# Top-k attention with a SMeLU MLP: the scores of two steps in one visit, with the values of two steps between them

## The chip, the cores and the metric

One core of one Trainium2 chip runs the whole program. The metric is the device time of one execution in microseconds (us). The kernel before has a median of 1504.06 us over three runs (1502.19 to 1506.8).

The engines named below each run their own queue of instructions in order: TensorE (PE for matmuls, PEld for weight loads), VectorE (DVE), ScalarE (ACT), GpSimd (POOL) and SyncE (SP), which here issues all the DMAs.

## The reference

```python
B, H, S, D = 8, 8, 576, 64                      # q, k, v: float32, (B, H, S, D)
scores = (1 / sqrt(D)) * q @ k.T                # per batch and head, (S, S)
kth    = np.partition(scores, -32)[..., -32]    # the 32nd largest of each row
scores = np.where(scores >= kth, scores, -1e9)
attn   = exp(scores - rowmax);  attn /= attn.sum(-1) + 1e-9
x      = (attn @ v).transpose(0, 2, 1, 3).reshape(4608, 512)
h      = x @ w_in                               # (512, 2048)
g      = h if h >= 1, 0 if h <= -1, else (h + 1)**2 / 4
out    = g @ w_out                              # (2048, 512)
```

## The kernel before

**Steps and rounds.** The unit of attention work is a *step*: a tile of queries and two heads, so two blocks of 128 rows of 576 scores. A query tile (a *round*) has four steps, one for each pair of heads. A batch has four tiles of 128 queries and a tail of 64; the tails of two batches are handled in rounds of two steps, each with four heads. Eight batches make 144 steps. Four steps fill one `xT` tile of 128 tokens by 512 features (a *chunk*), 36 in all, on which the MLP runs.

**One step.** TensorE multiplies queries by keys into two PSUM buffers (`scores`, L354), ScalarE evicts each half into `s` in SBUF with the scale (L355). VectorE finds the 32nd largest of each row: it folds each row into the larger and the smaller of two halves (`more`, `less`, L368), takes eight maxima at a time (L388, L416, L424, L435, L442) and strikes them out (L375). ScalarE makes the negative row maximum (`nmax`, L389) and the exponentials (L391) of the next step while VectorE works on this one. VectorE multiplies the exponentials by the mask and sums them (L454). GpSimd divides by the sum (L407). The weights then have to be turned for the second matmul: in the first eight steps and the last two TensorE does that (`transpose_w`, with `diag`, L404 and L469), in all others DMAs do (`move_w`): ScalarE splits the words into `halves` (L484), one DMA stores them as `rows` (L486), a transposing DMA brings them back as `wT` (L488). `values` multiplies `wT` by the values (L502, L510) and ScalarE copies the result into `xT` (L515, L517).

**The MLP.** `hidden` makes two blocks of 128 hidden units (eight matmuls, L535); ScalarE and GpSimd apply the activation (L539, L546, L551 to L553); `final` accumulates into `py` (L558). These pieces wait in the list `pending` and are put between the attention's instructions by `advance`.

**Early and late.** During the first eight steps (`early`) the weights are still converted to their form in SBUF, in slots of the same loop. The switch to the late order is at step 8.

**What sets the order.** The order on TensorE, VectorE, ScalarE and GpSimd is that in which the program calls the functions; only the queue of SP is ordered by the framework. The loop `for m in range(n + 2)` (L737) has seven slots for each step m. In slot 2 of an even late step the pending `hidden` pieces are drained, the values of steps m - 4 and m - 3 are made (`values_until`), and then the scores of step m + 2 (`begin_at`, L792). An odd late step makes only the scores of step m + 2. So TensorE leaves the MLP for attention twice in two steps. In slot 3 the weights of step m - 1 are moved. `advance` takes MLP pieces by a planned time for TensorE and VectorE.

**Queries and keys.** `queries(m + 3)` (L795) prepares a round's queries: for batches 0 and 1 TensorE transposes them, later `turn` (L275) does it as for the weights: ScalarE splits `q_in` into `parts`, a DMA stores `lines`, a transposing DMA fills `qT`. Then the load of the round after the next is issued into the buffer just read (two buffers `q_in`). The keys of the next batch come in the same way, one block every second step (`turned_keys_of`, `load_block`), each load issued ahead of the turn of the block before it (two buffers `k_in`); the keys of batches 0 and 1 are transposed by TensorE (`keys_of`, `load_keys`). Values come in by twelve loads for each batch (`load_values`, L194, L197, L202).

**Buffers that matter here.** `scores_of` and `weights_of` have three tiles each, taken by m modulo 3. PSUM tag `a` (scores, transposes) has two buffers, tag `ph` (hidden units, values) three, `py` one. `halves` has one buffer, `wT` four.

Of the kernel before, what the change touches and what calls it, by code (L numbers as in the profile page):

```python
# [11 lines left out]
F32 = mybir.dt.float32  # L12
# [10 lines left out]
LARGEST = 3.4028234e38  # L23
# [3 lines left out]
def kernel(  # L27
# [10 lines left out]
    nc = tc.nc  # L38
    B, H, S, D = q.shape
# [46 lines left out]
            nc.gpsimd.memset(x, 0.0)  # L86


    scores_of, weights_of = [[const.tile([P, 2, S + 8], F32, name=f"{x}{i}") for i in range(3)] for x in ("s", "e")]
    for i in range(3):  # L90
        nc.gpsimd.memset(scores_of[i][:, :, S:S + 1], LARGEST)
        nc.gpsimd.memset(weights_of[i][:, :, S:S + 1], 1e-9)

# [80 lines left out]
    def run(ctx, paired):  # L176
# [29 lines left out]

        def load_queries(b, t):
            if t < NT:
                q_in = stage.tile([P, H, D], F32, name="q_in", bufs=2)
                nc.sync.dma_start(out=q_in, in_=whole(q, b)[:, :, t, :])  # L210
            else:
                q_in = stage.tile([TL, H, D], F32, name="q_tl", tag="q_in", bufs=2)
                nc.sync.dma_start(out=q_in, in_=q[b, :, SM:S, :].rearrange("h p d -> p h d"))
            return q_in

# [18 lines left out]
        def keys_of(b):  # L234

            kT = stage.tile([P, NHP, S], F32, name="kT")
            k_tl = stage.tile([TL, H, D], F32, name="k_tl", bufs=1)
            got = dict(kT=kT)

            def load_keys(hp):  # L240
                k_in = stage.tile([P, NT, 2, D], F32, name="k_in")
                for j in range(2):
                    nc.sync.dma_start(out=k_in[:, :, j, :], in_=whole(k, b)[:, 2 * hp + j])
                return k_in

            k_in = load_keys(0)
            nc.sync.dma_start(out=k_tl, in_=k[b, :, SM:S, :].rearrange("h p d -> p h d"))
            yield got
            for hp in range(NHP):
                k_next = load_keys(hp + 1) if hp + 1 < NHP else None  # L250
                pt = ps.tile([P, NT, P], F32, name="pk", tag="a", bufs=2)
                for c in range(NT):
                    nc.tensor.transpose(pt[:, c, :], k_in[:, c].rearrange("p j d -> p (j d)"), ident)
                for j in range(2):
                    d = slice(j * D, (j + 1) * D)
                    copy = nc.vector.tensor_copy if b == 0 and hp < 2 and j else nc.scalar.copy
                    copy(kT[d, hp, main(j)], pt[d].rearrange("p c n -> p (c n)"))  # L257
                if hp == 0:
                    pt = ps.tile([P, NHP, TL], F32, name="pkt", tag="a", bufs=2)
                    for h2 in range(NHP):  # L260
                        nc.tensor.transpose(pt[:, h2, :], k_tl[:, 2 * h2:2 * h2 + 2].rearrange("p j d -> p (j d)"),
                                            ident[0:TL, 0:TL])
                    for j in range(2):
                        d = slice(j * D, (j + 1) * D)
                        copy = nc.vector.tensor_copy if b == 0 and j else nc.scalar.copy
                        copy(kT[d, :, tail(j)], pt[d])
                k_in = k_next
                if hp == NHP - 2:
                    loads = load_values(b)
                    got["v"], got["v_tl"] = next(loads)  # L270
                    for _ in loads:
                        pass
                yield got
# [16 lines left out]
        def turned_keys_of(b):  # L290

            kT = stage.tile([P, NHP, S], F32, name="kT")
            got = dict(kT=kT)

            def load_block(c):
                x = stage.tile([P, H, D], F32, name="k_block", tag="k_in")
                ends = k[b, :, SM:S, :].rearrange("h p d -> p h d")
                if c < NT:
                    nc.sync.dma_start(out=x[:, 0::2, :], in_=whole(k, b)[:, 0::2, c, :])
                    nc.sync.dma_start(out=x[TL:P, 1::2, :], in_=whole(k, b)[0:P - TL, 1::2, c, :])  # L300
                else:
                    nc.sync.dma_start(out=x[0:TL, 0::2, :], in_=ends[:, 0::2, :])
                nc.sync.dma_start(out=x[0:TL, 1::2, :], in_=whole(k, b)[P - TL:P, 1::2, c - 1, :] if c else ends[:, 1::2, :])
                return x

            blocks = {0: load_block(0)}
            got["loads"] = load_values(b)
            got["v"], got["v_tl"] = next(got["loads"])
            yield got
            for c in range(NT + 1):  # L310
                if c < NT:
                    blocks[c + 1] = load_block(c + 1)
                n = P if c < NT else TL
                turn(blocks.pop(c)[0:n], kT[:, :, c * P:c * P + n])
                yield got

        def turned_queries_of(q_in, t):
# [17 lines left out]

        def scores(st):
            t, hp, kT, qT = st["t"], st["hp"], st["keys"]["kT"], st["qT"]
            st["all"] = (scores_of[st["m"] % 3][:, :, 0:S + 1], weights_of[st["m"] % 3][:, :, 0:S + 1])
            st["s"], st["e"] = s, _ = [x[:, :, 0:S] for x in st["all"]]
            for hf in range(2):  # L340
                sp = ps.tile([P, 2, BANK], F32, name="sp", tag="a", bufs=2)
                c0, c1 = hf * SH, (hf + 1) * SH
                products = []
                for i in range(2):
                    for j in ([i] if t < NT else [0, 1]):
                        d = slice(j * D, (j + 1) * D)
                        g = hp if t < NT else hp + i
                        o = sp[:, i] if t < NT else sp[part(i, j), i]
                        products.append([(o[:, a0 - c0:a1 - c0], qT[d, g, :], kT[d, g, k0:k0 + a1 - a0])
                                         for a0, a1, k0 in pieces(i, j, c0, c1)])  # L350
                for some in zip_longest(*products):
                    for x in some:
                        if x is not None:
                            nc.tensor.matmul(*x, start=True, stop=True)  # L354
                nc.scalar.activation(s[:, :, c0:c1], sp[:, :, 0:SH], AF.Copy, scale=SCALE)  # L355
# [324 lines left out]
        def queries(m):  # L680
            nonlocal pe_time
            if m < n and steps[m][0:2] not in qTs:
                r = steps[m][0:2]
                if r[0] > 1:
                    qTs[r] = turned_queries_of(q_ins[r], r[1])
                else:
                    qTs[r] = queries_of(q_ins[r], r[1], nc.vector.tensor_copy if m == 0 else nc.scalar.copy)
                    pe_time += 0.5
                fetch(rounds.index(r) + 2)

        def begin(m):
            b, t, hp, ch, col = steps[m]
# [5 lines left out]
        def begin_at(m):  # L698
            nonlocal pe_time
            if m < n:  # L700
# [2 lines left out]
                pe_time += 1.15  # L703
                scored[m] = pe_time + 2.0

        for i in range(2):
            load(words, i)
        next(first)
        for i in range(2, len(room) or 2):
            load(words, i)  # L710
        fetch(1)
        queries(0)
        convert(12.0)
        begin_at(0)
# [22 lines left out]
        for m in range(n + 2):  # L737
# [22 lines left out]
            for slot in range(SLOTS):  # L760
# [26 lines left out]
                if slot == 2 and not early:  # L787
                    if m % 2 == 0:
                        while pending and taken is not None and taken.__name__ == "hidden" and take():
                            pass  # L790
                    values_until((m - 2) // 2 * 2)
                if slot == (4 if early else 2):  # L792
                    begin_at(m + 2)
                if slot == (6 if early else 1):
                    queries(m + 3)  # L795
                    if (m < n and prep is None and next_keys < B and steps[m][0] == next_keys - 1 and steps[m][1] >= 1
                            and (next_keys > 1 or converted == n_pieces)):
                        prep = (turned_keys_of if next_keys > 1 else keys_of)(next_keys)
                    if prep is not None and (m % 2 == 0 or next_keys == 1):
                        got = next(prep, None)  # L800
                        pe_time += 0.5 if next_keys < 2 else 0.0
                        if got is None:
                            prep, next_keys = None, next_keys + 1
                        else:
                            keys[next_keys] = got
                            value_loads = got.get("loads", value_loads)
                    elif value_loads is not None:
                        next(value_loads, None)
# [57 lines left out]
```

## Time and profile before

| what | value |
|---|---|
| median of three runs | 1504.06 us |
| profiled execution, its own time | 1504.76 us |
| its span, first to last instruction | 1503.0 us |
| mean granted clock of TensorE | 0.989 |
| PE busy | 1451.9 us, 97% |
| VectorE busy | 1413.6 us, 94% |
| ScalarE busy | 1159.2 us, 77% |
| GpSimd busy | 905.5 us, 60% |
| chain that ended last, by engine | PE 85%, DVE 6%, ACT 4% |

A busy share is an average over the span. Matmuls overlap, and their ends in the profile are modelled, so a full PE is not by itself a PE at its peak. A row of a timeline gives start, duration, engine, line of the kernel, operation, what is written from what is read with its shape, the number of instructions merged, and in brackets the idle time of the engine just before, with what ended it. A row of the waits gives who waited, for whom, the total in us, the number of times, and the longest.

### The profile page before, as it was taken

The page shows a single profiled execution, that of the slowest core. Times are in us where ns is not written, and L with a number is a line of the kernel's source. Part 1 is how long each engine was busy: PE and PEld are TensorE (multiplying, and loading weights), DVE is VectorE, ACT ScalarE, POOL GpSimd, SP SyncE. Part 2 cuts the span into 40 slices and gives each one's busy share as a digit, 9 for nine tenths or more (in the row PEclk, how much of TensorE's full clock was granted, in tenths as well). Part 3 has the DMA queues.
Part 4 walks back from the last instruction along what each step waited for, and adds up shares of the span by engine and source line. Part 5 has one row for each costly group of instructions (what it writes and reads, how often), then busy time and mean ns, then how long its engine had stood idle before and what let it go on. Part 6 is the DMA issues. An engine that isn't in the chain of part 4 may idle for free.

```text
span 1503.0 us, 32202 instructions
## 1 busy us (share of the span) xinstructions
PE 1451.9 (97%) x10755; PEld 1043.6 (69%) x10755; DVE 1413.6 (94%) x4392; ACT 1159.2 (77%) x2221; POOL 905.5 (60%) x1309
## 2 busy tenths in 40 slices
PE   6998899999999999999999999899999999999998
PEld 5665577677777777677777777667777777777675
DVE  6999999999999999999999999999999999999912
ACT  7986877777888887787778888678778888787632
POOL 3473466666666666566666666566666666666630
PEclk8999999999999999999999999999999999999999
DMA  8633667775677776776677887886667777655610
GB/s 253 203 116 106 166 162 197 193 185 165 169 197 186 200 196 189 211 191 177 161 195 197 194 201 172 198 223 184 164 188 186 201 186 180 169 159 140 144 24 17
DMA packets 510319, 260.94 MB, mean 174 GB/s; under 512 B 460992, under 2 KB 469184, under 8 KB 510144
## 3 DMA queue, kind: packets, MB, share of 16 engines
q1 hardware_dynamic: 510144, 258.80, 66.3%
q8 instruction: 87, 1.43, 0.4%
q14 instruction: 88, 0.72, 0.1%
HBM read 62.91 MB, written 102.63 MB: 110 GB/s over the span
## 4 chain that ended last, share of the span: by engine, by line
PE 85%; DVE 6%; ACT 4%; DMA 2%; issue 2%; POOL 0%; SPq 0%; ACTq 0%; POOLq 0%
PE ph L535 31%; PE py L558 31%; PE sp L354 10%; PE po L502 9%; DVE more L375 1%; PE po L510 1%; DMA rows<-halves 1%; PE pw L469 1%; DVE e L454 1%; DMA wT<-rows 1%; DVE more L368 1%; ACT halves L484 1%; ACT e L391 1%; ACT units L146 1%; DVE tops L416 0%
## 5 line engine op out<-in xcount | busy, mean ns | idle before, releaser
L535 PEld LDWEIGHTS ph<-xT,w_in 128*128 128x128 f32 x4608 | 547.4, 192 | 100.5 <-issue 78.0
L535 PE MATMUL ph<-xT,w_in 128*128 128x128 f32 x4608 | 556.8, 276 | 1.7 <-ACT xT L515 1.0
L558 PE MATMUL py<-w_out,g 128*128 128x512 f32 x1152 | 555.6, 602 | 1.0 <-ACT y L561 0.9
L551 POOL TENSOR_SCALAR r<-r 128x256 f32<-128x256 f32 x276 | 142.9, 518 | 453.9 <-ACT r L539 453.8
L375 DVE MATCH_REPLACE8 more<-tops,more 128x288 f32<-128x288 f32 x864 | 375.0, 437 | 0.0
L558 PEld LDWEIGHTS py<-w_out,g 128*128 128x128 f32 x1152 | 194.9, 190 | 166.4 <-issue 159.1
L484 ACT COPY halves<-e 128x1152 uint16<-128x1152 uint16 x268 | 293.6, 1143 | 15.6 <-DMA rows<-halves 15.6
L454 DVE SCALAR_TENSOR_TENSOR e<-s,kth,e 128x577 f32<-128x577 f32 x288 | 260.4, 939 | 2.6 <-ACT e L391 2.5
L553 POOL TENSOR_TENSOR g<-r,g 128x256 f32<-128x256 f32 x280 | 239.5, 855 | 22.0
L407 POOL TENSOR_SCALAR e<-e,rz 128x576 f32<-128x576 f32 x268 | 222.8, 841 | 13.4 <-DVE rz L400 13.4
L391 ACT ACTIVATE e<-s,nmax 128x576 f32<-128x576 f32 x288 | 222.6, 773 | 4.7
L539 ACT ACTIVATE r<-ph,half 128x256 f32<-128x256 f32 (+1 forms) x296 | 135.9, 459 | 116.0 <-PE ph L535 91.9
L355 ACT ACTIVATE s<-sp 128x576 f32<-128x576 f32 x288 | 171.9, 648 | 58.5 <-PE sp L354 57.1
L552 POOL TENSOR_TENSOR r<-r 128x256 f32<-128x256 f32 x276 | 191.0, 692 | 23.0
L354 PE MATMUL sp<-kT,qT 64*128 64x288 f32 x1024 | 163.1, 435 | 10.7 <-ACT kT L257 8.5
L502 PEld LDWEIGHTS po<-wT,v_in 128*64 128x64 f32 x2048 | 116.2, 139 | 61.1 <-ACT g L546 49.5
L502 PE MATMUL po<-wT,v_in 128*64 128x128 f32 x2048 | 141.3, 280 | 12.0 <-ACT g L546 8.6
L354 PEld LDWEIGHTS sp<-kT,qT 64*128 64x128 f32 x1024 | 89.5, 188 | 71.9 <-ACT r L539 29.6
L546 ACT ACTIVATE g<-ph,minus 128x256 f32<-128x256 f32 x280 | 130.0, 464 | 0.0
L416 DVE MAX8 tops<-more 128x8 f32<-128x288 f32 x288 | 125.4, 442 | 0.0
L368 DVE TENSOR_TENSOR more<-s 128x576 f32<-128x576 f32 x144 | 112.4, 781 | 12.3 <-ACT s L355 12.3
L368 DVE TENSOR_TENSOR less<-s 128x576 f32<-128x576 f32 x144 | 121.6, 845 | 0.0
(90 smaller groups left out, 1379.8 us busy)
## 6 DMA issues: line engine op xcount, KB each, us to landing
rows<-halves SPq DMA_DIRECT2D x134, 576.0 KB, 3.1
lines<-parts SPq DMA_DIRECT2D x48, 256.0 KB, 2.6
q_in<-in_q_dram SPq DMA_DIRECT2D x32, 256.0 KB, 3.9
v_in<-in_v_dram SPq DMA_DIRECT2D x32, 256.0 KB, 4.2
out_dram<-y SPq DMA_DIRECT2D x32, 256.0 KB, 2.9
raw<-in_moe_w_in_dram SPq DMA_DIRECT2D x32, 256.0 KB, 3.2
raw<-in_moe_w_out_dram SPq DMA_DIRECT2D x32, 256.0 KB, 3.3
kT<-in_moe_w_in_dram SPq DMA_DIRECT2D x8, 512.0 KB, 5.3
```

Of the source, the lines that this page charges most:

```text
L354: nc.tensor.matmul(*x, start=True, stop=True)
L368: nc.vector.tensor_tensor(out=x, in0=s[:, :, 0:SH], in1=s[:, :, SH:S], op=op)
L375: nc.vector.match_replace(out=st["rest"][:, i, :], in_to_replace=eight(st["tops"], i, r - 8), in_values=src[:, i, :], imm_value=LOWEST)
L391: nc.scalar.activation(e[:, i, :], s[:, i, :], AF.Exp, bias=nmax[:, i:i + 1])
L407: nc.gpsimd.tensor_scalar(st["e"][:, i, :], st["e"][:, i, :], rz[:, i:i + 1], 1.0, ALU.mult, ALU.mult)
L454: nc.vector.scalar_tensor_tensor(out=st["all"][1][:, i, :], in0=st["all"][0][:, i, :], scalar=last[i], in1=st["all"][1][:, i, :], op0=ALU. ...
L484: nc.scalar.copy(halves[:, :, i * S:(i + 1) * S], st["e"][:, i, :].bitcast(U16).rearrange("p (k t) -> p t k", t=2))
L502: nc.tensor.matmul(po[j * D:(j + 1) * D], v_in[:, h, c, :] if c < NT else v_tl[0][:, h, :], wT[:, block(j, c)], start=(c == 0), stop=(c == ...
L535: nc.tensor.matmul(ph[:, i], w_in[:, kk, f * P:(f + 1) * P], xT[:, kk], start=(kk == 0), stop=(kk == NK - 1))
L552: nc.gpsimd.tensor_tensor(out=r, in0=r, in1=r, op=ALU.mult)
L553: nc.gpsimd.tensor_tensor(out=g, in0=r, in1=g, op=ALU.add)
L558: nc.tensor.matmul(py[0], gs[f // group][:, f % group], w_out[:, f, :], start=(f == 0), stop=(f == NF - 1))
```

## The change

In a late step of even number the scores of step m + 2 are made first, then the values of two steps, then the scores of step m + 3; a late step of odd number makes none. A step's scores can then be written while those of three others are in use, so `scores_of` gets a fourth tile; `weights_of` keeps three. To find the room, `q_in` and `k_in` get one buffer each in place of two: a round's queries are turned two steps earlier (`queries(m + 5)`), the load issued after a turn is that of the next round and not of the one after it, and a key block is loaded after the turn of the block before it. For batch 0 the blocks of keys are loaded into `xT` tiles, which are not yet in use.

```diff
-    scores_of, weights_of = [[const.tile([P, 2, S + 8], F32, name=f"{x}{i}") for i in range(3)] for x in ("s", "e")]
+    scores_of, weights_of = [[const.tile([P, 2, S + 8], F32, name=f"{x}{i}") for i in range(bufs)]
+                             for x, bufs in (("s", 4), ("e", 3))]
...
-                q_in = stage.tile([P, H, D], F32, name="q_in", bufs=2)
+                q_in = stage.tile([P, H, D], F32, name="q_in", bufs=1)
...
             def load_keys(hp):
-                k_in = stage.tile([P, NT, 2, D], F32, name="k_in")
+                if b == 0:
+                    k_in = xtp.tile([P, NK, P], F32, name="xT").rearrange("p c (j d) -> p c j d", j=2)
+                else:
+                    k_in = stage.tile([P, NT, 2, D], F32, name="k_in", bufs=1)
...
-                k_next = load_keys(hp + 1) if hp + 1 < NHP else None
+                k_next = load_keys(hp + 1) if hp + 1 < NHP and b == 0 else None
...
-                k_in = k_next
+                k_in = load_keys(hp + 1) if hp + 1 < NHP and b else k_next
...
-                x = stage.tile([P, H, D], F32, name="k_block", tag="k_in")
+                x = stage.tile([P, H, D], F32, name="k_block", tag="k_in", bufs=1)
...
+                n = P if c < NT else TL
+                turn(blocks.pop(c)[0:n], kT[:, :, c * P:c * P + n])
                 if c < NT:
                     blocks[c + 1] = load_block(c + 1)
-                n = P if c < NT else TL
-                turn(blocks.pop(c)[0:n], kT[:, :, c * P:c * P + n])
...
-            st["all"] = (scores_of[st["m"] % 3][:, :, 0:S + 1], weights_of[st["m"] % 3][:, :, 0:S + 1])
+            st["all"] = (scores_of[st["m"] % 4][:, :, 0:S + 1], weights_of[st["m"] % 3][:, :, 0:S + 1])
...
-                fetch(rounds.index(r) + 2)
+                fetch(rounds.index(r) + 1)
...
+        def begin_until(m):
+            for x in range(len(state), m + 1):
+                begin_at(x)
...
-        fetch(1)
         queries(0)
...
+                    begin_until(min(m + 2, len(state)))
                     values_until((m - 2) // 2 * 2)
-                if slot == (4 if early else 2):
+                    begin_until(m + 3 - m % 2)
+                if slot == 4 and early:
                     begin_at(m + 2)
                 if slot == (6 if early else 1):
-                    queries(m + 3)
+                    queries(m + (3 if early else 5))
```

More of the change, by code (lines that the diff above doesn't have):

```diff
@@ L86 @@
             nc.gpsimd.memset(x, 0.0)
-    scores_of, weights_of = [[const.tile([P, 2, S + 8], F32, name=f"{x}{i}") for i in range(3)] for x in ("s", "e")]
-    for i in range(3):
-        nc.gpsimd.memset(scores_of[i][:, :, S:S + 1], LARGEST)
-        nc.gpsimd.memset(weights_of[i][:, :, S:S + 1], 1e-9)
+    scores_of, weights_of = [[const.tile([P, 2, S + 8], F32, name=f"{x}{i}") for i in range(bufs)]
+                             for x, bufs in (("s", 4), ("e", 3))]
+    for tiles, behind in ((scores_of, LARGEST), (weights_of, 1e-9)):
+        for x in tiles:
+            nc.gpsimd.memset(x[:, :, S:S + 1], behind)
     SPLIT = TOP_K // 2
@@ L208, in load_queries @@
             if t < NT:
-                q_in = stage.tile([P, H, D], F32, name="q_in", bufs=2)
+                q_in = stage.tile([P, H, D], F32, name="q_in", bufs=1)
                 nc.sync.dma_start(out=q_in, in_=whole(q, b)[:, :, t, :])
             else:
-                q_in = stage.tile([TL, H, D], F32, name="q_tl", tag="q_in", bufs=2)
+                q_in = stage.tile([TL, H, D], F32, name="q_tl", tag="q_in", bufs=1)
                 nc.sync.dma_start(out=q_in, in_=q[b, :, SM:S, :].rearrange("h p d -> p h d"))
```

## The prediction

> **What bounds the kernel now.** I read the engine totals first, then the same totals cut into stretches, then the list of waits, then the timelines of the engines over one pair of steps, last the stalls and the tail. The profiled execution took 1504.76 us (span 1503.0 and 1.8 around it); the median of the runs is 1504.06, so what I subtract from one holds for the other.
>
> Totals and two stretches (columns: window, its length, busy us of PE, PEld, DVE, ACT, POOL, granted clock, DMA share, GB/s):
>
> ```profile
> PE 1451.9 (97%) x10755; PEld 1043.6 (69%) x10755; DVE 1413.6 (94%) x4392; ACT 1159.2 (77%) x2221; POOL 905.5 (60%) x1309
> ...
> 400.00:600.00 200.00, 199.89 (x1498) 143.66 (x1497) 200.00 (x627) 164.59 (x313) 132.72 (x190) 1.00 0.76 195
> 800.00:1000.00 200.00, 194.46 (x1504) 140.06 (x1502) 195.29 (x608) 158.78 (x299) 125.28 (x182) 0.98 0.80 196
> ```
>
> Two engines are full at once in the steady state, TensorE and VectorE. Neither waits for the other. So I ask which one could go faster alone. VectorE's period is read from the starts of its first operation on a step's scores (`more<-s`): step 31 starts at 332.67 and step 59 at 600.66, 9.57 us a step; steps 100 to 140 give 9.57 too. The shortest steps, which repeat in every round of four, take 9.14. TensorE's period, from scores block to scores block four steps on, is 38.27 us = 4 x 9.57. Here is one pair's visit on TensorE, the odd step's scores after it, and VectorE and POOL at one spot:
>
> ```profile
> 703.55 1.02 PE L558 MATMUL py<-w_out,g 128*128 128x512 f32 x2
> 704.62 1.09 PE L502 MATMUL po<-wT,v_in 128*64 128x128 f32 x16
> 706.63 0.39 PE L502 MATMUL po<-wT,v_tail 128*64 128x128 f32 x4
> 706.95 1.24 PE L354 MATMUL sp<-kT,qT 64*128 64x288 f32 x8
> 708.12 1.12 PE L558 MATMUL py<-w_out,g 128*128 128x512 f32 x2
> 709.08 1.95 PE L535 MATMUL ph<-xT,w_in 128*128 128x128 f32 x16
> 714.46 1.24 PE L354 MATMUL sp<-kT,qT 64*128 64x288 f32 x8
> ```
> ```profile
> 697.00 1.27 DVE L454 SCALAR_TENSOR_TENSOR e<-s,kth,e 128x577 f32<-128x577 f32 x1
> 715.70 0.81 DVE L454 SCALAR_TENSOR_TENSOR e<-s,kth,e 128x577 f32<-128x577 f32 x1
> ```
> ```profile
> 696.53 1.12 POOL L553 TENSOR_TENSOR g<-r,g 128x256 f32<-128x256 f32 x1
> 705.46 0.73 POOL L553 TENSOR_TENSOR g<-r,g 128x256 f32<-128x256 f32 x1
> ```
>
> TensorE has no hole to speak of: its own work fills 38.27. VectorE's masked multiply takes 0.81 alone and 1.27 where POOL's add (0.73 alone, 1.12 here) lies over it. That stretch, 0.4 to 0.5 us an overlap, is all that separates 9.14 from 9.57. While TensorE was ahead, from step 13 (160.67) to step 24 (265.34), VectorE made 9.52 a step. So I take TensorE as the pace and VectorE as a follower that would take only 0.05 us less if it were let.
>
> The waits that VectorE does have, and one of their causes:
>
> ```profile
> DVE more L368 <- ACT s L355: 12.3, 7, 2.8
> PEld po L502 <- ACT g L546: 49.5, 51, 6.2
> ```
> ```profile
> 615.55 4.02 SPq L202 DMA_DIRECT2D v_tail<-in_v_dram  x6
> ```
> ```profile
> 622.75 2.21 ACT L484 COPY halves<-e 128x1152 uint16<-128x1152 uint16 x2 [2.66 <-DMA rows<-halves]
> ```
> ```profile
> 626.41 1.80 PE L502 MATMUL po<-wT,v_in 128*64 128x128 f32 x16 [2.81 <-ACT g L546]
> ```
> ```profile
> 632.44 0.98 DVE L368 TENSOR_TENSOR more<-s 128x576 f32<-128x576 f32 x1 [2.73 <-ACT s L355]
> ```
>
> Read down: six issues for value tails hold SP's queue 4 us, the store of `rows` goes out late, ScalarE waits to refill its one `halves` buffer, the hidden units' evictions queue behind that, the values find no PSUM buffer, and the scores that stand behind the values reach VectorE late. It happens once more at 978 (TensorE 5.41, VectorE 2.81).
>
> The tail decides who is paid:
>
> ```profile
> 1428.43 0.69 ACT L404 ACTIVATE diag<-ident,rz 128x128 f32<-128x128 f32 x2 [1.51 <-DVE seconds L442]
> ```
>
> TensorE waits 2.13 us for this `diag`, which waits for VectorE's last step; the 74 us from there to the end are the same instructions in both kernels. So only time that VectorE gains moves the end.
>
> **What the Trainium skill says.** *TensorEngine Tiling (Array Packing)*, Key Properties: changing the tiling mode, not just the tile, drains TensorE. The trace agrees: scores (64-row tiles), values (64-column tiles) and MLP (whole array) follow each other with holes of 0.10 us and more, worked out below. *GPSIMD Engine Reference*, Key points: POOL shares its SBUF interfaces with VectorE and contends with VectorE instructions that have two SBUF inputs. The trace agrees (1.27 against 0.81). *Perfetto Trace Analysis*, Optimization Strategy: repeated bubbles can mean too few buffers; here the one 1 us hole before `po` (51 times) is a PSUM buffer awaited.
>
> **The change, part by part.**
>
> *Order on TensorE.* In the instruction order of the two programs a pair was: values, values, scores, MLP, scores, MLP; it becomes scores, values, values, scores, MLP. The MLP matmuls between visits are the same in number (80 and 14, then 48 and 18, hidden and output). One second-layer matmul recurs every 0.43 us, so the two of 703.55 would be over at 704.41: MLP to values costs 0.21 here (0.10 at 683.54 to 684.50). Values to scores: four tails take 0.22, over at 706.85, scores at 706.95: 0.10. Scores to MLP: 708.12 to 709.08 is 0.96 for 0.86 of work: 0.10. MLP to scores the same 0.10. Before: 0.10 to 0.21 + 0.10 + 0.10 + 0.10 + 0.10 = 0.50 to 0.61. After: three of 0.10 and one scores-to-values, which no trace shows; between 0 and 0.20 (a drain with the next weights exposed), I take 0.10 as for its neighbours. Saved 0.10 to 0.21, with the unknown 0 to 0.31; I take 0.15 x 66 pairs = 10 us of TensorE, 0.08 a step. That allows 9.49; VectorE's free rate, 9.52, is met first. Over the 128 steps from 13 to 141: 0.05 x 128 = **-6.4 us**, 0 if it stays at 9.57, -10 if all passes.
>
> *Scores ahead of the values.* At both stalls the even step's scores no longer stand behind the late values; the odd step's come some 8 us earlier than now. Scores are ready 1.9 us before use at the tightest (708.93 for 710.82); that becomes 4.2 by the values' 2.33 us. The stall itself stays, I assume: the value-tail loads still come four in a row. Removed: 2.73 + 2.81 = **-5.5**; the two steps after each stall are long by 3.7 in all (10.97, 9.79, 10.98, 10.25 against 9.57), half of which I credit: **-1.9**. TensorE's lost time is covered by its new lead; without that cover the 8 us come back.
>
> *Evictions.* The second scores need both PSUM buffers of tag `a` free: first eviction 0.8 after its matmuls' start, both done by 2.0 (706.95, 708.94); the second scores start 1.17 + 2.33 = 3.5 later. Hidden, unless ScalarE is over 1.5 us behind. ScalarE's row maximum and exponentials of the next step now stand behind two more evictions at even steps: the second exponential, done at 712.61, comes near 714.2 and is wanted at 716.43 (the first 715.70). Hidden with 1.5 to 2 us to spare. Odd steps lose two evictions and gain the same. The fourth scores buffer lets this be written while VectorE still reads three; the memset of its guard column is 0.1 us in the lead-in.
>
> *Queries.* The turn (ScalarE copy 1.04, store, load of the next tile, DMA transpose of 1.25 on SP) moves two steps earlier at the same slot, once in four steps; SP issues the same number. With one `q_in` the next load waits for that copy, which the old load of the same buffer did too. It has four steps (two at the tails) for 3.9 us: nothing.
>
> *Key blocks.* Three issues (1.6 to 2.5 us of SP) move from ahead of the turn to behind its copy. SP would hold the `rows` store and `wT` behind them if the copy were late; the store of `lines` waits for that same copy already, so nothing. Landing 4 us, need 19 us later.
>
> *Start.* Batch 0 keys go to `xT` tiles, so all four blocks load at once, and a query load leaves the queue: no wait of VectorE shown there is on them; 0, between -2 and +2. At the switch (step 8) one query transpose and its copy (0.66 and 0.56) come ahead of the scores for which VectorE already waits 2.04: **+1.2**. Single `k_in` for batch 1: a block must land within about 5 us of TensorE work; 0, at worst +3.
>
> Sum: -6.4 - 5.5 - 1.9 + 1.2 = -12.6, 1504.76 to 1492.2; from the median 1491.5. I say 1492.
>
> **Rivals.**
> *Only the waits go* (VectorE stays at 9.57): -5.5 - 1.9 + 1.2 = -6.2, 1498. For: 100% busy. Against: 9.52 while TensorE was ahead.
> *Nothing arrives*: the loads' burst holds ScalarE longer and VectorE waits for exponentials in place of scores (it did so 0.61 and 1.90 at the stalls): +2.5 at each of three batches and no rate: 1504.
> *Slower: more overlap with POOL.* All hidden work now comes in one block a pair, so POOL's operations land elsewhere on VectorE's two-input operations. Price 0.43 each. The gain is gone at 12.6 / 0.43 = 29 more overlaps, one in 4.4 steps. One in two steps costs 27.5 in place of the 6.4 gained: 1504.76 - 6.2 + 27.5 = 1526; one in four about 1512. For: POOL is 60% busy, VectorE's two-input work is 2.8 us a step, phases are chance. Against: at present three steps in four are hit already.
>
> **How the numbers follow.** Forecast 0.42, waits only 0.20, nothing arrives 0.16, slower 0.22. Range: from the full TensorE saving, all of the waits and a faster start (-10 - 5.5 - 3.7 - 2 = -21.2, 1483) to one overlap in four steps, 1512. About 4.5 us (0.3%) is what this kernel's measurement can tell from no change. Faster takes the first two, 0.62; same 0.16; slower 0.22.
>
> **What would show it.** Right: scores blocks directly either side of the values; steps of 9.5; no wait of VectorE for scores at the late batches; a longer wait of TensorE for `diag` in the tail. Wrong: VectorE 100% busy with steps of 9.65 or more and more masked multiplies over 1.2 us (slower rival); waits of the masked multiply for the exponentials; or waits for `wT` before the values.

## The result, and the profile after

The changed kernel takes 1492.86 us (median of six runs, 1490.03 to 1493.44). On the same chip the kernel before takes 1507.13 us (six runs, 1502.19 to 1510.69). The ratio is 0.9906, 95% interval 0.9886 to 0.9926: 14 us less, inside the range and faster, as forecast. The three runs of before that the prediction started from lie toward the fast end of what that kernel does, and so does its profiled execution; between the two profiled spans (1503.0 and 1490.9) the difference is 12.1 us, and the accounts below are made of those 12.1. They compare one profiled execution of each kernel, so a difference of one us or so in a stretch may be chance. The mean granted clock of the two is 0.989 and 0.991; if the whole span went with it, that would be 3 us of the 12 (an estimate), but the steady steps below show no such gain.

The page of the changed kernel, engine totals and the shares of the chain that ended last:

```profile
PE 1437.7 (96%) x10755; PEld 1044.0 (70%) x10755; DVE 1411.9 (95%) x4392; ACT 1157.7 (78%) x2221; POOL 949.8 (64%) x1310
...
PE 65%; DVE 13%; ACT 10%; DMA 5%; POOL 4%; issue 3%; SPq 0%; POOLq 0%; ACTq 0%; DVEq 0%
```

TensorE does the same instructions in 14.2 us less busy time (1451.9 before), and its share of the chain falls from 85% to 65%. Two stretches of the changed kernel in the view by windows (columns as before: busy us of PE, PEld, DVE, ACT, POOL):

```profile
400.00:600.00 200.00, 197.30 (x1491) 142.69 (x1490) 200.00 (x626) 161.62 (x309) 141.83 (x189) 1.00 0.75 196
1000.00:1200.00 200.00, 200.00 (x1451) 145.47 (x1452) 200.00 (x637) 163.76 (x314) 132.37 (x193) 1.00 0.77 191
```

From 400 to 600 us VectorE is still full and TensorE now has holes (197.30 where it had 199.89): TensorE has become the faster of the two there. From 1000 to 1200 us both are still full. But the step did not shorten. I read it from the starts of `more<-s` as the prediction did, and cut the whole execution at the same steps in both kernels:

| stretch, by the start of `more` of these steps | before, us | after, us | difference |
|---|---|---|---|
| start to step 13 | 160.67 | 160.13 | -0.5 |
| steps 13 to 61 | 459.13 | 460.53 | +1.4 |
| steps 61 to 66 (first stop) | 52.78 | 49.19 | -3.6 |
| steps 66 to 97 | 296.99 | 298.11 | +1.1 |
| steps 97 to 100 (second stop) | 35.78 | 29.68 | -6.1 |
| steps 100 to 143 | 411.55 | 410.68 | -0.9 |
| step 143 to the end (tail) | 86.1 | 82.6 | -3.5 |

The gain is at two places of some thirty to fifty us and in the tail. The steady steps, 122 of 144, give nothing: 9.59, 9.62 and 9.55 us after, against 9.57, 9.58 and 9.57.

What the two stops look like now. The queue of SP, then ScalarE, in the timeline of the changed kernel near 615 us, the first stop:

```profile
612.49 2.60 SPq L203 DMA_DIRECT2D v_tail<-in_v_dram  x4
615.18 0.54 SPq L490 DMA_DIRECT2D rows<-halves  x1
```
```profile
618.71 2.21 ACT L488 COPY halves<-e 128x1152 uint16<-128x1152 uint16 x2 [1.38 <-DMA rows<-halves]
```

Before, six issues of value tails stood in a row for 4.02 us, and ScalarE waited 2.66. The six were the last two of one batch and the four of the next; SP's queue is ordered by the framework, and in the changed kernel it came out as four and four, with stores of `rows` between them. At the second stop, first before and then after, four tails stand ahead of the store in both kernels:

```profile
967.00 2.65 SPq L202 DMA_DIRECT2D v_tail<-in_v_dram  x4
974.36 2.20 ACT L484 COPY halves<-e 128x1152 uint16<-128x1152 uint16 x2 [4.75 <-DMA rows<-halves]
```
```profile
960.63 2.61 SPq L203 DMA_DIRECT2D v_tail<-in_v_dram  x4
966.87 2.21 ACT L488 COPY halves<-e 128x1152 uint16<-128x1152 uint16 x2 [1.02 <-DMA rows<-halves]
```

ScalarE's wait falls from 4.75 us to 1.02 there for three reasons: the store is issued 4.5 us after ScalarE has filled `halves` in place of 5.9, it lands 3.5 us later in place of 4.5, and ScalarE comes to its next copy after 7.0 us in place of 5.8. VectorE's waits at the stops before were 2.73 and 2.81 us for scores and 0.61 and 1.90 for exponentials; all four are gone, and TensorE's longest hole at the stops is 1.5 us, where it had 2.81 and 5.41. From the waits of the changed kernel:

```profile
PE sp L358 <- ACT s L359: 14.6, 18, 3.9
ACT halves L488 <- DMA rows<-halves: 12.5, 8, 2.8
PEld po L506 <- ACT g L550: 9.5, 20, 1.7
DVE more L372 <- ACT s L359: 8.3, 6, 2.8
```

The waits of the weight load for the values (`PEld po <- ACT g`) were 49.5 us in 51 places and are 9.5 in 20. VectorE's six waits for scores all lie before 151 us; none is left at the stops. The first of these rows is new: TensorE waits for the evictions of the first scores before it can write the second. ScalarE's waits for the store are fewer by 3 us in all and not gone: near the first stop there are now four, of 1.1 to 1.8 us, where there were two, of 0.5 and 2.66.

The tail. ScalarE before, which the prediction did not show, and after:

```profile
1422.25 0.27 ACT L515 COPY xT<-po 128x128 f32<-128x128 f32 x1 [0.83 <-PE po L502]
1422.41 0.21 ACT L389 ACTIVATE nmax<-tops 128x2 f32<-128x2 f32 x1
```
```profile
1409.87 0.27 ACT L519 COPY xT<-po 128x128 f32<-128x128 f32 x1 [0.83 <-PE po L506]
1410.50 0.21 ACT L393 ACTIVATE nmax<-tops 128x2 f32<-128x2 f32 x1 [0.37 <-DVE tops L392]
...
1416.53 0.69 ACT L408 ACTIVATE diag<-ident,rz 128x128 f32<-128x128 f32 x2 [1.52 <-DMA rows<-halves]
```

The last step's row maximum `nmax` needs `tops`, which VectorE has written 2.1 us after the start of its `more` in both kernels (its maxima start 1.3 us after it and take 0.8). Before, `nmax` comes 5.5 us after that `more` (1422.41 for 1416.90), straight behind two copies `xT<-po` that had waited for TensorE's values. After, it comes at 2.2 (1410.50 for 1408.33), and its row names VectorE's `tops`. The exponentials, `halves`, the store and the turned rows follow from it. So before, the tail was started by TensorE, through ScalarE's queue; after, by VectorE. The fourteen kernels of this document agree: in five `nmax` comes 2.2 us after the last `more`, and their tails last 82.1 to 83.2 us; in the other nine it comes after 3.8 to 8.2 us, and they last 85.9 to 89.1.

### The profile page after: what moved, and what is told of

It reads as the page before. It is cut to its first block, busy times and chain, and to the rows that moved or that the text cites. A ratio compares the mean times of both kernels' runs of the same rounds, so it can differ in the third digit from the quotient of the medians.

```text
span 1490.9 us, 32088 instructions
## 1 busy us (share of the span) xinstructions
PE 1437.7 (96%) x10755; PEld 1044.0 (70%) x10755; DVE 1411.9 (95%) x4392; ACT 1157.7 (78%) x2221; POOL 949.8 (64%) x1310
## 4 chain that ended last, share of the span: by engine, by line
PE 65%; DVE 13%; ACT 10%; DMA 5%; POOL 4%; issue 3%; SPq 0%; POOLq 0%; ACTq 0%; DVEq 0%
PE py L562 26%; PE ph L539 23%; PE sp L358 8%; PE po L506 6%; DVE more L379 3%; ACT halves L488 2%; DVE e L458 2%; DMA rows<-halves 2%; ACT e L395 2%; POOL r L556 2%; DMA wT<-rows 2%; ACT r L543 1%; DVE more L372 1%; POOL g L557 1%; DVE tops L420 1%
## 5 line engine op out<-in xcount | busy, mean ns | idle before, releaser
L562 PE MATMUL py<-w_out,g 128*128 128x512 f32 x1152 | 542.3, 597 | 0.7 <-ACT y L565 0.7
L555 POOL TENSOR_SCALAR r<-r 128x256 f32<-128x256 f32 x276 | 172.4, 625 | 401.3 <-ACT r L543 401.3
L562 PEld LDWEIGHTS py<-w_out,g 128*128 128x128 f32 x1152 | 199.5, 191 | 165.1 <-issue 159.8
L411 POOL TENSOR_SCALAR e<-e,rz 128x576 f32<-128x576 f32 x268 | 251.6, 949 | 10.0 <-DVE rz L404 10.0
L458 DVE SCALAR_TENSOR_TENSOR e<-s,kth,e 128x577 f32<-128x577 f32 x288 | 252.5, 912 | 0.5 <-ACT e L395 0.4
L557 POOL TENSOR_TENSOR g<-r,g 128x256 f32<-128x256 f32 x280 | 221.0, 789 | 22.0
L556 POOL TENSOR_TENSOR r<-r 128x256 f32<-128x256 f32 x276 | 201.6, 730 | 23.0
L506 PE MATMUL po<-wT,v_in 128*64 128x128 f32 x2048 | 138.3, 276 | 6.4 <-DMA wT<-rows 5.6
L372 DVE TENSOR_TENSOR more<-s 128x576 f32<-128x576 f32 x144 | 122.5, 850 | 8.3 <-ACT s L359 8.3
L420 DVE MAX8 tops<-more 128x8 f32<-128x288 f32 x288 | 125.4, 443 | 0.0
L392 DVE MAX8 tops<-more 128x8 f32<-128x288 f32 x288 | 116.4, 443 | 0.0
```

Of the source, the lines that this page charges most:

```text
L411: nc.gpsimd.tensor_scalar(st["e"][:, i, :], st["e"][:, i, :], rz[:, i:i + 1], 1.0, ALU.mult, ALU.mult)
L458: nc.vector.scalar_tensor_tensor(out=st["all"][1][:, i, :], in0=st["all"][0][:, i, :], scalar=last[i], in1=st["all"][1][:, i, :], op0=ALU. ...
L506: nc.tensor.matmul(po[j * D:(j + 1) * D], v_in[:, h, c, :] if c < NT else v_tl[0][:, h, :], wT[:, block(j, c)], start=(c == 0), stop=(c == ...
L555: nc.gpsimd.tensor_scalar(r, r, 1.0, 0.0, ALU.min, ALU.max)
L556: nc.gpsimd.tensor_tensor(out=r, in0=r, in1=r, op=ALU.mult)
L557: nc.gpsimd.tensor_tensor(out=g, in0=r, in1=g, op=ALU.add)
```

## The experiments

The theories. *T1*, the recorded one: TensorE set the pace, the new order frees it, VectorE then runs at 9.52. *T2*: the steady rate is VectorE's with GpSimd beside it, and the gain is the two stops and the tail. Inside T2, two causes for the stops: the order of the scores, or the loads (SP's queue).

**GpSimd's share left out.** In both kernels:

```diff
-                else:
+                elif converted < n_pieces:
                     nc.gpsimd.tensor_scalar(r, r, 1.0, 0.0, ALU.min, ALU.max)
                     nc.gpsimd.tensor_tensor(out=r, in0=r, in1=r, op=ALU.mult)
-                nc.gpsimd.tensor_tensor(out=g, in0=r, in1=g, op=ALU.add)
+                if converted < n_pieces:
+                    nc.gpsimd.tensor_tensor(out=g, in0=r, in1=g, op=ALU.add)
```

> The kernel before, with GpSimd's three operations on each hidden block left out once the weights are converted (the output lacks the quadratic part of the activation). Question: what sets the 9.57 us of a step. If TensorE is the pace (the prediction's reading), VectorE's operations shrink to their undisturbed 9.14 but steps stay at 9.5 to 9.57, VectorE now waits for scores in most steps, and TensorE's period stays 38.1 to 38.3 for four. If VectorE stretched by GpSimd is the pace, steps fall to 9.2 to 9.3 and TensorE keeps up. Time: about 1495 to 1505 under the first, about 1465 under the second.

> The changed kernel with the same operations left out. If TensorE is the pace, its period for four steps shows what the fewer changes between kinds of matmul are worth: the prediction says 0.2 to 0.6 us less than in the same kernel with the order before (take 37.8), steps of 9.45, with VectorE waiting for scores. If VectorE is the pace, both kernels without these operations have the same steps of 9.2.

Measured, one run each: before 1503.01 us (span 1501.2), changed 1482.41 (span 1480.6). Steps 100 to 140 take 9.574 and 9.422 us. The waits of the kernel before without that work:

```profile
DVE more L368 <- ACT s L355: 50.7, 51, 2.4
```

VectorE, relieved, mostly waits for scores: in the kernel before TensorE can go no faster than 4 x 9.574 = 38.3 us for four steps. In the changed order four steps take 4 x 9.422 = 37.7, with no idle time on TensorE in that stretch, so TensorE's saving is 0.6 us for two pairs, 0.3 a pair. And the changed kernel would be some 10 us faster without this part of GpSimd's work, the kernel before only 2 (span). So T1 is right that TensorE limits the kernel before and that the new order frees it, and wrong about what VectorE makes of it.

The reason can be counted on VectorE's operations with two inputs in SBUF: the two masked multiplies of a step (0.81 us undisturbed), `more` and `less` (0.74) and the scan that finds `kth` (0.20). What they take beyond that, in us a step, beside the length of the step:

| steps | beyond, before | beyond, after | step, before | step, after |
|---|---|---|---|---|
| 13 to 61 | 0.43 | 0.46 | 9.57 | 9.59 |
| 66 to 97 | 0.44 | 0.48 | 9.58 | 9.62 |
| 100 to 143 | 0.43 | 0.41 | 9.57 | 9.55 |

Without GpSimd's work it is 0.03 and 0.05 in steps 13 to 61. The Trainium skill's *GPSIMD Engine Reference*, Key points, says that GpSimd contends with VectorE instructions of two SBUF inputs; these are such instructions, and here it costs some 0.4 us a step in both kernels. VectorE has no idle time in these steps in either kernel, so the step is its undisturbed 9.14 and this stretch. In the kernel before, TensorE needs as long; after, only VectorE does.

**Order alone.** The kernel before, its buffers and loads, with the even step's scores ahead of the values:

```diff
+                    begin_at(m + 2)
                     values_until((m - 2) // 2 * 2)
-                if slot == (4 if early else 2):
+                if slot == 4 and early:
                     begin_at(m + 2)
```

> The kernel before with one exchange: at an even late step the scores of step m + 2 come ahead of the values of two steps; still one step's scores per visit, three scores buffers, the old loads. If the gain is that VectorE no longer stands behind late values at the two stalls, this gives most of it: 8 to 10 us less than before, with no wait of VectorE for scores at 632 and 984. If the gain came from the merged visit, the fourth buffer or the moved loads: within 3 us of before.

Measured: 1509.67 us, ratio 1.002 (1.0008 to 1.0031). By the table's cuts, against before: steps 61 to 66 -1.6, 97 to 100 -6.0. This order takes 7.7 us from the stops although the stores are issued nearly as late as before: 5.5 and 5.8 us after ScalarE has filled `halves`, with eight and three value tails right ahead of them, where it was 6.7 and 5.9. ScalarE waits 1.46 and 0.48 us for them; at the second stop it comes to its next copy 2.7 us later than before, and the store lands 1.4 us sooner. The kernel gives the 7.7 back: +2.6 in steps 13 to 61, +4.8 in 66 to 97, +1.0 in the tail. Whether part of the 6.0 at the second stop is only the same wait taken earlier, in the 4.8 just ahead of it, is not told apart. Its waits have rows that neither kernel has near the top:

```profile
PE sp L354 <- DMA qT<-lines: 8.4, 7, 2.6
...
PE sp L354 <- DMA qTt<-lines: 2.4, 3, 1.2
```

Scores that come sooner need turned queries sooner, and these are still turned for step m + 3 only.

**The same with early queries.** One edit more: `queries(m + (3 if early else 5))`.

> The kernel before with the scores of the even step put ahead of the values (as in the run with this edit alone) and, besides, the queries of a batch's next tile turned two steps earlier, as the change does it; buffers of scores, query and key loads stay those of before. Theory A (the order of the scores lost its gain to TensorE's wait for turned queries, 8.4 us in that run's trace): the wait is gone and the total comes down by 8 to 12 us, to 1496 to 1502 us. Theory B (the fourth scores buffer and two scores in one visit are needed): within 3 us of before, 1504 to 1510 us.

Measured: 1495.17 us, ratio 0.9915 (0.9900 to 0.9929), somewhat below theory A's range; the row for `qT` is gone from the waits. Theory A holds. In its profile, the slowest of its four executions, the stops give -3.5 and -6.6. This edit also makes the row of eight tails into four and four on SP, so how much of the 14.5 us between the two runs is the queries and how much the tails is not told apart. With three buffers of scores and one step a visit this is within the interval of the changed kernel: most of its gain does not need two steps in a visit.

**New buffers and loads, old order.** The changed kernel, with `values_until` ahead of one `begin_at(m + 2)` in each visit, as before:

```diff
-                    begin_until(min(m + 2, len(state)))
                     values_until((m - 2) // 2 * 2)
-                    begin_until(m + 3 - m % 2)
+                    begin_at(m + 2)
```

> The changed kernel's buffers, loads and early queries, with the scores in the order of before: values of two steps ahead of the scores of the odd step, the scores of each step in its own visit. Theory A (the gain at the two stops is the loads', the steady rate is the order's): steps as before, 9.56 to 9.60 us, the stops smaller by some 8 us together, total 1497 to 1501 us. Theory B (the order of the scores makes the gain): 1505 us or more. Theory C (as when the values go ahead of both scores, TensorE loses more than 0.15 us per step): above 1510 us.

Measured: 1502.24 us, ratio 0.9968 (0.9956 to 0.9980): 5 us less than before, 9 more than the changed kernel. The time lies between the numbers of theories A and B. The stops give -1.3 and -5.2, the tail nothing. So the loads alone and the order alone each take most of the second stop and little of the first; together they take most of both. The tail does not follow from the loads alone.

**Values ahead of both scores.** The changed kernel without its first `begin_until`, so that the two steps' scores follow each other:

> The changed kernel with the two values ahead of both scores, all else as changed: the visit is still merged. If the stalls are the gain, they come back (waits of VectorE for scores near 630 and 980), and the time is 6 to 11 us above the changed kernel, near that of before. If the merged visit is the gain, at most 3 us above the changed kernel, plus up to 68 times 1.3 us of TensorE where the second scores wait for the first ones' eviction with nothing between them.

Measured: 1520.57 us, ratio 1.012 (1.0083 to 1.0158). Its waits:

```profile
PEld sp L358 <- ACT s L359: 70.3, 134, 4.3
PE sp L358 <- ACT s L359: 25.4, 65, 3.8
DVE more L372 <- ACT s L359: 17.8, 27, 2.8
```

TensorE waits 65 times, 25.4 us in all, until the first scores are evicted and their PSUM buffers free for the second. Steps become 9.79, 9.74, 9.77. The stops do not come back (-4.2 and -5.3), although the values stand ahead of the scores again; but here every step is longer. Two steps in one visit pay only with the values between them: the same work in the other order costs 28 us.

**The tails' loads left out.** `range(2)` becomes `range(2 if b < 2 else 0)` for the first pair of loads, and the others stand under `if b < 2`. The expectations name the third and fourth batch; left out are the value tails of the third batch and all later ones.

> The kernel before, without the loads of the value tails for the third and fourth batch (six transfers each that SyncE issues in a row at 615 us and five near 970 us; the tail rows of the values of those batches are then those of an earlier batch). Theory A (the two long stops near 620 and 970 us come from this burst, which holds SyncE for some 4 us each and with it the stores of the weights and the loads behind them): the late steps at 61 to 66 and 97 to 100 shrink by 2.5 to 5 us each, total 6 to 10 us less, 1497 to 1501 us against 1507. Theory B (the stops come from TensorE's and ScalarE's own work in the preparation of a batch's keys, whatever SyncE does): within 2 us of before.

> The changed kernel without the same loads of the value tails for the third and fourth batch. Theory A (the change has already taken the burst apart, by the order of SyncE's transfers): 0 to 2 us less than the changed kernel, 1490.5 to 1493 us. Theory B (the order of the scores protects VectorE from a stop that is still there): TensorE still stops, and taking the burst away brings 3 us or more, below 1490 us.

Measured: before 1492.38 us, ratio 0.9901 (0.9868 to 0.9935); changed 1489.59, ratio 0.9888 (0.9855 to 0.9921). The wait that stood at the head of the stop, in the kernel before and in the same kernel without the tails:

```profile
ACT halves L484 <- DMA rows<-halves: 15.6, 7, 4.8
```
```profile
ACT halves L485 <- DMA rows<-halves: 0.7, 2, 0.5
```

Taking thirty-six short loads out of SP's queue brings the kernel before to the changed kernel's time, with steps of 9.62, 9.55, 9.57. The stops give -4.4 and -6.7, the tail -3.9 (`nmax` 2.2 us after `more`, as in the changed kernel). In the changed kernel the same edit brings 3 us, with intervals that overlap; its stops shrink by 1.6 more, and 1.8 of the profiled difference is in the start.

**The tails on GpSimd's queue.** All loads made, those of the tails from the third batch on issued by GpSimd: `(nc.gpsimd if b > 1 else nc.sync).dma_start(...)`.

> The kernel before with the value tails of the third batch and all later ones loaded by GpSimd's queue instead of SyncE's; every load is still made. Theory A (the stops near 620 and 970 us come from the six transfers in a row on SyncE): as without these loads, 1490 to 1496 us. Theory B (the bytes or the memory traffic of the tails cause the stops, or GpSimd's issuing costs VectorE as much): 1500 us or more.

> The changed kernel with the value tails of the third batch and all later ones loaded by GpSimd's queue. Theory A (SyncE's issue of the tails is all that they cost): as without these loads, 1489 to 1491 us, 2 to 3 us less than the changed kernel. Theory B (issuing on GpSimd delays its part of the hidden blocks, or VectorE): 1493 us or more.

Measured: before 1495.11 us, ratio 0.9911 (0.9896 to 0.9925); changed 1494.62, ratio 0.9914 (0.9896 to 0.9933). In the kernel before the stops give -3.6 and -6.6 and ScalarE's wait for the store falls to 1.4 us in all: it is the place in SP's queue that costs, not the bytes. In the changed kernel there is nothing left to gain by it; theory B's number came, but with this interval I cannot say that GpSimd's issuing costs anything.

**The last `diag` in a buffer of its own.** `tag="raw" if late else "halves"` in the changed kernel:

> The changed kernel with the diagonal of the last step in a buffer of its own, so that VectorE does not wait for the store of the weights that were in it (1.52 us in the changed kernel's trace). Theory A (the end is one chain through this wait): 1.5 us less, 1491.3 us. Theory B (the weights' store or the last turned rows end the tail all the same): within 0.5 us of the changed kernel, 1492.5 to 1493.3 us.

Measured: 1495.64 us, ratio 0.9916 (0.9886 to 0.9945). ScalarE in its timeline:

```profile
1411.62 0.21 ACT L393 ACTIVATE nmax<-tops 128x2 f32<-128x2 f32 x1
...
1416.03 0.68 ACT L408 ACTIVATE diag<-ident,rz 128x128 f32<-128x128 f32 x2
```

`diag` no longer waits for the store. But here TensorE's values were late (1409.00 for VectorE's 1407.79), `nmax` came 3.8 us after `more`, and TensorE then waited 2.50 us for turned rows: the tail lasts 86.0 us, as in the kernel before. Neither theory's number came, since the tail began later. It fits theory B's picture, that the turned rows end the tail, and they start from `nmax`; it does not show what the wait for `diag` is worth alone.

**Two buffers of `halves`.** The changed kernel with three buffers of scores and one step a visit (even scores ahead of the values), and the room given to a second `halves` (the last step's `diag`, which shares that buffer, gets the second one too):

> The room of the fourth buffer of scores is given to a second buffer of the weights on their way to memory (halves); loads and early queries are the changed kernel's, the scores of each step are computed in a visit of their own, those of the even step ahead of the values. Theory A (what stopped the kernel before is ScalarE's wait for the store of the one halves buffer, and the order alone, without the fourth buffer, does as well as the change where queries come early): ScalarE's waits for that store are near zero and the total is 1489 to 1494 us, at or below the changed kernel. Theory B (two scores in one visit and the fourth buffer carry the gain): 1498 us or more.

Measured: 1495.91 us, ratio 0.9944 (0.9922 to 0.9965; nine runs, 1490.77 to 1502.49). ScalarE's waits for the store are gone from the list, the stops give -4.5 and -6.7, and at step 143 VectorE is 4.5 us ahead of the changed kernel; the tail takes it back (`nmax` 5.75 us after `more`, 87.4 us to the end). The time lies between the two theories' numbers. The waits and the stops went as A said; the tail again depends on where TensorE stands when VectorE finishes. The three runs with the new order and one step a visit all have a long tail (86.9 to 87.5 us).

No version that computes everything was measured below the changed kernel; those nearest to it lie within its interval.

## Why the prediction was right, and where not

The time (1492 for 1492.86) and the sum (-12.6 for -12.1 between the spans) are right. The parts of the sum are not, and that they add up is luck: the steady rate came out 8.0 us worse than forecast, and the stops, the start and the tail together 7.5 us better:

| step | predicted | measured |
|---|---|---|
| steady rate, TensorE's saving passed on | -6.4 | +1.6 |
| waits and long steps at the stops | -7.4 | -9.7 |
| start | +1.2 | -0.5 |
| tail | 0 | -3.5 |

**Order on TensorE.** TensorE could go no faster before, as said. The unknown switch from scores to values took what its neighbours take. A pair's visit in the timeline of the changed kernel:

```profile
717.24 1.24 PE L358 MATMUL sp<-kT,qT 64*128 64x288 f32 x8
718.41 1.09 PE L506 MATMUL po<-wT,v_in 128*64 128x128 f32 x16
...
720.74 1.24 PE L358 MATMUL sp<-kT,qT 64*128 64x288 f32 x8
721.91 2.05 PE L539 MATMUL ph<-xT,w_in 128*128 128x128 f32 x16
```

From the scores to the values 1.17 us, from the scores to the MLP 1.17 too, the same as before. The saving is 0.3 a pair, not 0.15 (37.7 for 38.3 us in the run without GpSimd's work; 37.8 in steps 107 to 123 of the changed kernel, where TensorE is full). Its half beyond the one switch less I have not traced to an instruction.

**The step that failed** is "VectorE's free rate, 9.52, is met first", and with it "VectorE as a follower". A follower waits, and VectorE did not: in the steady steps of the kernel before it has no idle time, and each step's scores are ready at least 1.4 us before `more` reads them (the prediction took 1.9 for the tightest). So scores that come sooner could not shorten its step. The 9.52 was read off eleven steps (13 to 24), too few to fix a rate that hangs on where GpSimd's operations fall. Over long stretches of the changed kernel the step is 9.55 to 9.62, VectorE's undisturbed 9.14 and 0.41 to 0.48 of contention, no better than before; the term of -6.4 came out at +1.6.

**Scores ahead of the values.** Right in direction: with the stores still late this order took 7.7 us from the stops where 7.4 were forecast, though that run lost as much elsewhere, in part just ahead of the second stop. Wrong is "the stall itself stays, I assume": TensorE's holes of 2.81 and 5.41 us are gone, and with them VectorE's waits for exponentials (2.5 us), which the sum did not count. The loads of the changed kernel alone, in the old order, are worth some 6.5 us at the stops; both together give 9.7, so they remove in part the same time. Which of the two makes how much of the 9.7 is not told apart.

**Evictions.** In effect hidden, though not as fully as said: from step 16 on TensorE waits for the first evictions at sixteen places, 0.2 to 1.4 us each, and VectorE never waits for scores there. Putting the values between the scores, and not ahead of both, is worth 28 us.

**Queries: nothing.** The turns cost nothing where they are. But the step missed that the new order needs them two steps earlier; without that, TensorE waits 10.8 us and nothing is gained. **Key blocks: nothing** was not tested alone; the run with the old key loads lies within the interval.

**Start.** The +1.2 came at its place: step 7 begins 0.9 us earlier than before, step 8 0.5 later. By step 12 it was gone again (1.0 earlier).

**Tail.** "Only time that VectorE gains moves the end" was wrong. I read the wait for `diag` and took VectorE to be behind it. `diag` needs both VectorE's sum and the `halves` buffer, whose store hangs on `nmax`, and `nmax` stood in ScalarE's queue behind copies that waited for TensorE. In the changed kernel TensorE is no longer late there, and that is worth 3.5 us. The new order is not the only way to it: in the old order without the tails' loads the tail gave 3.9.

**Rivals.** *Only the waits go* is nearer to what happened than the forecast: no rate, and the stops. Its 1498 lacks the rest of the stops and the tail. *Nothing arrives*: VectorE does not wait for exponentials at the stops (and its sum, -7.4 + 1.2 + 7.5, gives 1506, not 1504). *More overlap*: 0.46, 0.48 and 0.41 us a step for 0.43, 0.44 and 0.43, so the contention neither grew much nor fell; the two-input work that it lies over is 3.3 us a step undisturbed and 3.7 as it ran, not 2.8. Of the signs named, scores stand either side of the values, VectorE has no late wait for scores, and TensorE's wait for `diag` is longer (2.60 for 2.13); steps of 9.5 did not come.

## What to carry to other kernels

When two engines are both full, leave out some work of a third that contends with one of them before taking either as free to follow: it shows how far each could go alone. Here it showed that one engine's saving would be eaten by the other. And an engine without waits is not a follower. A stop with a long chain of waits is best traced to its head, here a few short loads ahead of a store in one DMA queue; several different edits made it smaller, and reordering the work behind it was one of them. An edit that changes only loads and buffers changes the order in a queue that a scheduler fills, so look at that queue's order too; and before calling a tail VectorE's, look at what stands ahead in the queue of the engine between.

## What the runs showed of the hardware

Issuing the same loads cost GpSimd as much as SP, 1.25 us for two (SP 2.60 for four), and left the stops as small as without the loads. The transposing DMA of a step's weights held SP for 2.6 us (median of the changed kernel; 2.3 at least), where the store of the same rows mostly took 0.3 to 0.5. And relieving VectorE of some 0.4 us a step brought the kernel before 2 us and the changed kernel 10: the contention was there in both, and what it cost depended on whether TensorE needed that time too.
